# Masks added by a scaled identity on TensorE, one reduction for both heads, and q and k copied by twos in the first 16 units

## The chip, the core and the metric

The kernel runs on one core of one Trainium2 chip. The core has a matrix engine, TensorE (PE in the profile, PEld for its weight loads), and three engines for elementwise work: VectorE (DVE), ScalarE (ACT) and GpSimd (POOL). SyncE (SP) issues most of the transfers. Each engine takes its instructions in a fixed order and stands still at one whose input isn't there. Matmuls write to PSUM, a memory of eight banks per partition; the other data lie in SBUF. The metric is the device time of one execution in microseconds (us), lower is better.

## The reference

Attention with 4 batches, 8 heads, 768 positions and 64 channels per head, then a feed-forward layer with a rational activation. Per head h, with rel = i - j:

```python
scores = q @ k.T / sqrt(64)
is_global = j < n_global;  is_local = (rel >= 0) & (rel < n_local)     # 8 and 96
dist = n_local where global and not local, else |rel|
scores = scores - 2.0 ** -(h + 1) * dist, and -1e9 where neither global nor local
a = softmax(scores);  x = a @ v                     # x: 3072 tokens x 512
hid = x @ w_in                                      # 512 x 2048
g = (a0 + a1 hid + a2 hid^2 + a3 hid^3) / (1 + |b0| |hid| + |b1| hid^2 + 1e-6)
out = g @ w_out                                     # 2048 x 512
```

The weights come as 64-bit numbers, so each piece of 128x512 is fetched as 512 KB and decoded on the chip.

## The kernel before

**The work.** The 24 row blocks of 128 tokens are taken two at a time, a chunk of 256 tokens (c). A *unit* u is one pair of heads (p) of one row block; a chunk has 8 units, four pairs of its first row block and then four of its second. Since only 96 positions back and 8 global ones count, a unit looks at its own key block and the one before it; row block 0 of a batch (i = 0) has only its own. So a unit's scores are 128 x 2 heads x 256 keys, or 128 x 2 x 128 where i = 0. Units 0 to 3 have i = 0, units 4 to 15 have i = 1 to 3. Beside the units run *feed-forward steps* f, eight to a chunk, each for 256 hidden channels.

**A unit below 24 (PLAIN)** goes through these stages:

- `st_load`: q and k of two units are fetched into one tile `nat`, v into `vt`.
- `st_qkT`: PE transposes q and k of one unit into a PSUM tile `tk` (L389).
- `st_qkE`: ACT copies them to SBUF: q per head into `qz`, in the half of the partitions that belongs to the head, zeros in the other half (L402, scaled by 2^(h-2)), and k into `kF` (L404); where i = 0 also the 8 global keys into `kGF` (L406).
- `st_score`: PE multiplies per head into a PSUM tile `s` (L433, in fp32, which the trace shows as two records per matmul). DVE then adds a mask to the scores of each head, scales by -2^-(h+1), writes the result to the SBUF tile `pr` and takes its minimum along the row into `stats`, in one operation per head (L452). The mask holds minus the distance, and -1e30 where a key does not count. POOL copies the global keys over the next block's first columns (L440).
- `st_soft`: ACT takes the exponential of `pr` in place, with the minimum as bias, and sums the row (L462).
- `st_sums`, `st_norm`: DVE adds and inverts (L467, L469); from unit 8 on POOL scales `pr` (L478). For units 0 to 7 the inverse goes through PE instead (L511) and is multiplied in `st_x`.
- `st_pT`: PE transposes the probabilities into `tp` (L494), ACT copies them to SBUF (L497). `st_pv`: PE multiplies them with v into `o`, two units at a time (L520); `st_x` writes x (L541, L542, and from unit 8 on L549, L550).

The tiles `tk`, `s`, `tp` and `o` share three PSUM banks. `pl.qz` has three buffers.

**Beside it**, 32 weight pieces are fetched (L183, into six raw buffers that a decoding frees) and decoded by ACT (L202), POOL (L206) and DVE (L207, L209). The hidden matmuls of the first chunk are L263, with two records each, those of later chunks L271; the activation is L295 to L318 on ACT, POOL and DVE, its last operation L318; the output matmuls of the first chunk are L342, of later ones L347. L222 and L223 split decoded weights into two parts for the later chunks.

**The order** is made at build time by a scheduler from the priorities in `PRI` and `PRI_A`, from an estimate of how long things take, and from which of the buffers is free. So an edit of the early units also moves what stands beside them, on every engine.

Of the kernel before, what the change touches and what calls it, by code (L numbers as in the profile page):

```python
# [18 lines left out]
P = 128  # L19
G = 8  # L20
# [86 lines left out]
def tile_kernel(ctx: ExitStack, tc: tile.TileContext, q, k, v, n_global, n_local,  # L107
# [255 lines left out]
    ident_r = const.tile([P, P], FR, name="ident_r")  # L363
    mask0 = const.tile([P, P], BF16, name="mask0")
    masks = const.tile([P, 3, P], BF16, name="masks")
    sp = {}
# [9 lines left out]
    def st_qkT(u):  # L376
        p = unit(u)[2]
        if u >= PLAIN:
            tk = pl.ps_t.tile([P, 2, 2, P], FR, tag="t", name=f"tk{u}")
            for y in range(2):  # L380
                for z in range(2):
                    n = nat[u // 2][:, 1 - z, 2 * y:2 * y + 2, :]
                    nc.tensor.transpose(out=tk[:, y, z, :], in_=n.rearrange("p a d -> p (a d)"), identity=ident_r)  # L383
                tqk[u + y] = tk[:, y]
            return
        tk = pl.ps_t.tile([P, 2, P], F32, tag="t", name=f"tk{u}")
        for z in range(2):
            n = nat[u // 2][:, z, 2 * (p % 2):2 * (p % 2) + 2, :]
            nc.tensor.transpose(out=tk[:, z, :], in_=n.rearrange("p a d -> p (a d)"), identity=ident)  # L389
        tqk[u] = tk  # L390
# [4 lines left out]
    def st_qkE(u):  # L395
        c, t, p, b, i = unit(u)
        tk = tqk.pop(u)
        if u < PLAIN:
            qz = pl.qz[:, u % 3]
            for x in range(2):  # L400
# [25 lines left out]
    def st_score(u):  # L426
        c, t, p, b, i = unit(u)
        qT = qTs.pop(u)
        s_ps = pl.ps_t.tile([P, 2, 2, P], F32, tag="t", name=f"s{u}")
        for x in range(2):  # L430
            h = 2 * p + x
            if u < PLAIN:
                nc.tensor.matmul(out=blocks_of(s_ps[:, x], i), lhsT=qT[:, x, :], rhs=blocks_of(pl.kF[:, p], i),  # L433
# [10 lines left out]

        def mask(x):
            m0, m = (mask0, masks) if u < PLAIN or x == 0 else (pl.half0, pl.halves)
            return m0 if i == 0 else m[:, 0:2, :] if i % 2 else m[:, 1:3, :]
        pr = pl.att.tile([P, 2, 2, P], F32, tag="prob", name=f"pr{u}")
        st = stats[:, u % 4]
        for x in range(2):  # L450
            h = 2 * p + x
            nc.vector.tensor_tensor_reduce(  # L452
                out=blocks_of(pr[:, x], i), in0=blocks_of(s_ps[:, x], i), in1=mask(x),
                scale=-(2.0 ** -(h + 1 if u < PLAIN else 2 * p + 1)), scalar=3e38, op0=ALU.add, op1=ALU.min, accum_out=st[:, x:x + 1])
        prob[u] = (pr, st)

    def st_soft(u):
        i = unit(u)[4]
        pr, st = prob[u]
        for x in range(2):  # L460
            d = blocks_of(pr[:, x], i)
            nc.scalar.activation(out=d, in_=d, func=AF.Exp, scale=-1.0, bias=st[:, x:x + 1],  # L462
                                 accum_out=st[:, 2 + 2 * x:3 + 2 * x])

# [63 lines left out]
    def st_x(u0):  # L528
# [15 lines left out]
        xh, xl = xT[c]  # L544
        if u0 < DIVIDED:
            rs = pl.early.tile([P, 2, P], F32, tag="rs", name=f"rs{u0}", bufs=1)
            nc.scalar.copy(out=rs, in_=r)
            nc.vector.tensor_tensor(out=o, in0=o, in1=rs, op=ALU.mult)
        nc.scalar.copy(out=xh[:, ps, cs], in_=o)  # L549
# [6 lines left out]
    def windowed(lates):  # L556
# [4 lines left out]
        pl.kGF = pl.early.tile([P, NPAIR, G], F32, name="kGF")  # L561
        pl.qz = pl.early.tile([P, 3, 2, P], F32, name="qz")
        nc.scalar.dma_start(out=ni[:, 0:2], in_=n_local.bitcast(I32).partition_broadcast(1))
# [30 lines left out]
        for t in range(NU + LAG + F2 + 1):  # L594
# [32 lines left out]
            if t == PLAIN:  # L627
# [3 lines left out]
                pl.kG = pl.late.tile([P, H, G], FR, name="kG")  # L631
                pl.halves = pl.late.tile([P, 3, P], BF16, name="halves")
                pl.half0 = pl.late.tile([P, P], BF16, name="half0")
                tc.cur_priority = base + 1000 * t
                for m, full_m in ((pl.halves, masks), (pl.half0, mask0)):
                    nc.vector.tensor_scalar(out=m, in0=full_m, scalar1=0.5, scalar2=None, op0=ALU.mult)
                on("split", st_move, t)
            ffn("ffn1a", st_ffn1, f, 0)
            if t < PLAIN or t % 2 == 0:
                on("qkT", st_qkT, t)  # L640
# [198 lines left out]
```

## Time and profile before

| | |
|---|---|
| median of 3 runs | 750.11 us (749.84 to 750.31) |
| the profiled execution, whole | 750.29 us |
| its span, first to last instruction | 748.4 us |
| mean granted TensorE clock | 0.996 |
| TensorE busy | 724.8 us, 97% of the span |
| VectorE, ScalarE, GpSimd busy | 601.4, 576.9, 456.4 us |

How to read the rows of the prediction. A row of the stretches gives its bounds and length, then the busy time and number of instructions of PE, PEld, DVE, ACT and POOL, then the granted clock as a share of the full one, the busy share of the DMA engines and GB/s. A row of a timeline gives start, length (us), engine, line, operation, what it writes and reads, and in brackets how long the engine had been idle ahead of it and what ended that. Lengths of neighbours overlap, so the distance of two starts is what an operation holds its engine for. A row of a group gives line, operation, form and count, then total busy time and the mean of one in ns. The chain is followed back from the last instruction, always to what released it. Numbers at the end of tile names are left out in the profile: `w_3f` stands for the decoded pieces (3, 0) to (3, 3) and 3.

### The profile page before, as it was taken

The page shows a single profiled execution, that of the slowest core. Times are in us where ns is not written, and L with a number is a line of the kernel's source. Part 1 is how long each engine was busy: PE and PEld are TensorE (multiplying, and loading weights), DVE is VectorE, ACT ScalarE, POOL GpSimd, SP SyncE. Part 2 cuts the span into 40 slices and gives each one's busy share as a digit, 9 for nine tenths or more (in the row PEclk, how much of TensorE's full clock was granted, in tenths as well). Part 3 has the DMA queues.
Part 4 walks back from the last instruction along what each step waited for, and adds up shares of the span by engine and source line. Part 5 has one row for each costly group of instructions (what it writes and reads, how often), then busy time and mean ns, then how long its engine had stood idle before and what let it go on. Part 6 is the DMA issues. An engine that isn't in the chain of part 4 may idle for free.

```text
span 748.4 us, 15330 instructions
## 1 busy us (share of the span) xinstructions
PE 724.8 (97%) x5026; PEld 629.8 (84%) x5026; DVE 601.4 (80%) x1437; ACT 576.9 (77%) x1303; POOL 456.4 (61%) x504
## 2 busy tenths in 40 slices
PE   5898999999999999999999999999999999999996
PEld 4575667888988989999999999998988989998995
DVE  5889965888889797878888888887888888876565
ACT  6898576977987886877877878777877877866674
POOL 3384996776576675665756657656666566664441
PEclk9999999999999999999999999999999999999999
DMA  9986101123534443334434334334434333210000
GB/s 259 306 277 224 48 22 23 50 52 99 146 103 126 151 121 94 113 108 101 119 94 120 113 101 125 107 101 106 124 93 124 117 86 107 74 50 1 29 1 33
DMA packets 123581, 79.49 MB, mean 106 GB/s; under 512 B 82532, under 2 KB 104036, under 8 KB 123492
## 3 DMA queue, kind: packets, MB, share of 16 engines
q1 hardware_dynamic: 122288, 77.89, 36.4%
q8 instruction: 42, 0.69, 0.4%
q10 hardware_dynamic: 1204, 0.52, 0.3%
q14 instruction: 47, 0.39, 0.2%
HBM read 35.92 MB, written 6.29 MB: 56 GB/s over the span
## 4 chain that ended last, share of the span: by engine, by line
PE 90%; DVE 3%; DMA 3%; ACT 1%; issue 1%; SPq 0%; POOL 0%; DVEq 0%; ACTq 0%
PE h L271 34%; PE acc L347 32%; PE o L520 5%; PE s L438 5%; PE tp L494 4%; PE acc L342 3%; PE h L263 3%; PE s L433 2%; PE tk L383 1%; DMA r<-in_moe_w_in_dram 1%; DMA r<-in_moe_w_out_dram 1%; PE tk L389 1%; DMA nat<-in_q_dram 0%; DVE pr L452 0%; ACT pr L462 0%
## 5 line engine op out<-in xcount | busy, mean ns | idle before, releaser
L478 POOL TENSOR_SCALAR pr<-pr,stats 128x256 f32<-128x256 f32 (+1 forms) x176 | 156.3, 899 | 74.8 <-DVE stats L469 42.7
L271 PE MATMUL h<-xh,win_l 128*128 128x256 f32 x704 | 198.2, 282 | 0.0
L304 POOL TENSOR_TENSOR fa<-fa,fs 128x512 f32<-128x512 f32 x95 | 123.5, 1300 | 98.0 <-ACT fs L297 85.3
L347 PE MATMUL acc<-wout_l,g 128*128 128x512 f32 x352 | 139.3, 396 | 0.0
L271 PEld LDWEIGHTS h<-xh,win_l 128*128 128x128 f32 x704 | 133.1, 189 | 2.1 <-issue 1.2
L327 POOL TENSOR_TENSOR g<-fu,g 128x512 fp32r<-128x512 f32 x87 | 113.9, 1310 | 34.2 <-ACT g L326 22.8
L295 ACT ACTIVATE fu<-h,coef 128x512 f32<-128x512 f32 (+1 forms) x97 | 74.9, 772 | 45.0 <-PE h L271 39.8
L462 ACT ACTIVATE pr<-pr,stats 128x256 f32<-128x256 f32 (+1 forms) x192 | 92.9, 487 | 16.8 <-DVE stats L452 16.0
L311 ACT ACTIVATE fs<-fa,coef 128x512 f32<-128x512 f32 (+1 forms) x97 | 69.6, 718 | 30.0 <-POOL fa L304 28.4
L316 DVE SCALAR_TENSOR_TENSOR fu<-fu,coef,q 128x512 f32<-128x512 f32 (+1 forms) x97 | 71.6, 738 | 24.7 <-ACT q L312 23.3
L302 DVE TENSOR_TENSOR fu<-fu,h 128x512 f32<-128x512 f32 (+1 forms) x97 | 65.7, 677 | 30.5 <-ACT fs L297 27.9
L347 PEld LDWEIGHTS acc<-wout_l,g 128*128 128x128 f32 x352 | 66.2, 188 | 11.9
L415 ACT ACTIVATE kq<-tk 64x256 fp32r<-64x256 f32 x144 | 54.2, 377 | 26.6 <-DVE kq L416 15.1
L303 DVE SCALAR_TENSOR_TENSOR fu<-fu,coef,h 128x512 f32<-128x512 f32 (+1 forms) x97 | 71.7, 739 | 2.0
L317 DVE SCALAR_TENSOR_TENSOR q<-fa,coef,q 128x512 f32<-128x512 f32 (+1 forms) x97 | 72.1, 744 | 0.0
L497 DVE COPY pT<-tp 128x512 f32<-128x512 f32 (+1 forms) x75 | 48.4, 646 | 26.0 <-PE tp L494 25.1
L416 DVE SCALAR_TENSOR_TENSOR kq<-tk,kq 64x256 fp32r<-64x256 f32 x144 | 60.8, 423 | 8.6 <-ACT kq L415 4.2
L318 DVE SCALAR_TENSOR_TENSOR fu<-q,fu 128x512 f32<-128x512 f32 (+1 forms) x97 | 66.1, 682 | 1.6
L297 ACT ACTIVATE fs<-h,coef 128x512 f32<-128x512 f32 (+1 forms) x97 | 66.2, 683 | 1.5 <-DMA out_dram<-o 1.2
L296 ACT ACTIVATE fa<-h,coef 128x512 f32<-128x512 f32 (+1 forms) x97 | 65.5, 675 | 0.4 <-DMA out_dram<-o 0.4
L326 ACT CAST g<-fu 128x512 fp32r<-128x512 f32 (+1 forms) x89 | 54.9, 617 | 8.5 <-DVE fu L318 7.8
L312 ACT ACTIVATE q<-fs 128x512 f32<-128x512 f32 (+1 forms) x97 | 57.3, 591 | 2.2 <-DVE fu L318 0.7
(258 smaller groups left out, 2006.1 us busy)
## 6 DMA issues: line engine op xcount, KB each, us to landing
pm<-pr SPq DMA_DIRECT2D x60, 256.0 KB
mv<-nat SPq DMA_DIRECT2D x36, 256.0 KB
qT<-kq SPq DMA_DIRECT2D x144, 64.0 KB
r<-in_moe_w_in_dram SPq DMA_DIRECT2D x16, 512.0 KB
r<-in_moe_w_out_dram SPq DMA_DIRECT2D x16, 512.0 KB
nat<-in_q_dram SPq DMA_DIRECT2D x48, 128.0 KB
vt<-in_v_dram SPq DMA_DIRECT2D x48, 128.0 KB
nat<-in_k_dram SPq DMA_DIRECT2D x46, 128.0 KB
```

The costliest lines, as they stand in the source:

```text
L271: nc.tensor.matmul(out=hps[f][:, y, :], lhsT=w[:, fs], rhs=x[:, ct, :], start=(n == 0), stop=(n == 3 * NCT - 1))
L295: nc.scalar.activation(out=u, in_=h, func=AF.Identity, scale=a3, bias=a2)
L297: nc.scalar.activation(out=s, in_=h, func=AF.Square, scale=b1)
L303: nc.vector.scalar_tensor_tensor(out=u, in0=u, scalar=a1, in1=h, op0=ALU.add, op1=ALU.mult)
L304: side(f).tensor_tensor(out=a, in0=a, in1=s, op=ALU.add)
L311: nc.scalar.activation(out=s, in_=a, func=AF.Ln, bias=q1)
L316: nc.vector.scalar_tensor_tensor(out=u, in0=u, scalar=a0, in1=r, op0=ALU.add, op1=ALU.mult)
L317: nc.vector.scalar_tensor_tensor(out=r, in0=a, scalar=q1, in1=r, op0=ALU.add, op1=ALU.mult)
L327: side(f).tensor_tensor(out=g[:, 1, ys], in0=u, in1=g[:, 0, ys], op=ALU.subtract)
L347: nc.tensor.matmul(out=acc, lhsT=gs[f][:, z, y, ts], rhs=w, start=(ft == 0 and n == 0), stop=(ft == NFT - 1 and n == 2))
L462: nc.scalar.activation(out=d, in_=d, func=AF.Exp, scale=-1.0, bias=st[:, x:x + 1], accum_out=st[:, 2 + 2 * x:3 + 2 * x])
L478: nc.gpsimd.tensor_scalar(out=d, in0=d, scalar1=st[:, 6 + x:7 + x], scalar2=None, op0=ALU.mult)
```

## The change

For units 0 to 15 (`MASKED`):

- A bf16 tile `slope` holds four times the identity, times -2^-(2p+1). Per unit PE runs one matmul of it with the masks, 512 columns (256 where i = 0), which starts the accumulation in `s`; the two score matmuls are added to it. The masks now lie twice, whole for the first head and halved for the second, so the two operations at turn 24 that made the halves go to the start. q is scaled by -0.125 for all heads.
- DVE takes the minima of both heads in one `tensor_reduce` over `s`. ACT's exponentials read `s` in PSUM and write `pr`; before, they read and wrote `pr`.
- Four transposes of two units go into one PSUM tile; ACT copies q of two units in one operation per head, and k in one. The global keys are copied by POOL, for two pairs at once. `pl.qz` has four buffers.
- Three lines in `st_x` are removed that no unit reached. Units from 16 on keep their operations; units 16 to 23 find their mask under a new index.

```diff
+MASKED = 16
...
+        if u < MASKED:
+            tk = pl.ps_t.tile([P, 2, 2, P], F32, tag="t", name=f"tk{u}")
+            for y in range(2):
+                for z in range(2):
+                    n = nat[u // 2][:, z, 2 * y:2 * y + 2, :]
+                    nc.tensor.transpose(out=tk[:, z, y, :], in_=n.rearrange("p a d -> p (a d)"), identity=ident)
...
+        if u < MASKED:
+            n = u % 4
+            for x in range(2):
+                ds_ = slice(x * D, (x + 1) * D)
+                nc.scalar.activation(out=pl.qz[ds_, n:n + 2, x, :], in_=tk[ds_, 0], func=AF.Copy, scale=-0.125)
+            nc.scalar.copy(out=pl.kF[:, p:p + 2, i % 2, :], in_=tk[:, 1])
+            if i == 0:
+                nc.gpsimd.tensor_copy(out=pl.kGF[:, p:p + 2, :], in_=pl.kF[:, p:p + 2, 0, 0:G])
...
+        if u < MASKED:
+            m = masks[:, :, 0:2, :] if i % 2 else masks[:, :, 1:3, :]
+            nc.tensor.matmul(out=s_ps if i else s_ps[:, :, 0, :], lhsT=pl.slope[:, p, :], rhs=m if i else mask0,
+                             start=True, stop=False)
...
+                nc.tensor.matmul(out=blocks_of(s_ps[:, x], i), lhsT=qT[:, x, :], rhs=blocks_of(pl.kF[:, p], i),
+                                 start=False, stop=(x == 1))
...
+        if u < MASKED:
+            W = 2 if i else 1
+            nc.vector.tensor_reduce(out=st[:, 0:2], in_=s_ps[:, :, 0:W, :].rearrange("p x w k -> p x (w k)"),
+                                    op=ALU.min, axis=mybir.AxisListType.X)
...
-            d = blocks_of(pr[:, x], i)
-            nc.scalar.activation(out=d, in_=d, func=AF.Exp, scale=-1.0, bias=st[:, x:x + 1],
-                                 accum_out=st[:, 2 + 2 * x:3 + 2 * x])
+            nc.scalar.activation(out=blocks_of(pr[:, x], i), in_=blocks_of(src[:, x], i), func=AF.Exp, scale=-1.0,
+                                 bias=st[:, x:x + 1], accum_out=st[:, 2 + 2 * x:3 + 2 * x])
...
+        for p in range(NPAIR):
+            nc.scalar.mul(out=pl.slope[:, p, :], in_=ident, mul=-(2.0 ** -(2 * p + 1)))
...
+        for m in (mask0, masks):
+            nc.vector.tensor_scalar(out=m[:, 1], in0=m[:, 0], scalar1=0.5, scalar2=None, op0=ALU.mult)
```

What the scheduler made of it is shown at three places. Line numbers in the changed kernel are one higher for the weights and the activation (L207, L209, L318 become L208, L210, L319), and 31 to 36 higher behind `st_score`.

**VectorE at the decoding of weight piece 7 (w_out).** The tile `m` and `w_7f` are its two decode steps, `xl` the low part of x for units 8 and 9, `stats` the sums of unit 11. Before:

```order
L318 SCALAR_TENSOR_TENSOR fu_608<-q_662,fu_608 128x512
L550 TENSOR_TENSOR xl_701<-o_690,xh_700 128x2x128
L207 SCALAR_TENSOR_TENSOR m_715<-m_715,r_7_713 128x512
L209 SCALAR_TENSOR_TENSOR w_7f<-r_7_713,m_715 128x512
L207 SCALAR_TENSOR_TENSOR w_8f<-w_8f,r_8_782 128x512
L207 SCALAR_TENSOR_TENSOR w_9f<-w_9f,r_9_789 128x512
L209 SCALAR_TENSOR_TENSOR w_8f<-r_8_782,w_8f 128x512
```

Now:

```order
L476 TENSOR_REDUCE stats<-s_706 128x2
L208 SCALAR_TENSOR_TENSOR m_696<-m_696,r_7_694 128x512
L582 TENSOR_TENSOR xl_682<-o_671,xh_681 128x2x128
L210 SCALAR_TENSOR_TENSOR w_7f<-r_7_694,m_696 128x512
L503 TENSOR_REDUCE stats<-stats 128x2
L505 RECIPROCAL stats<-stats 128x2
L208 SCALAR_TENSOR_TENSOR w_8f<-w_8f,r_8_765 128x512
```

Both decode steps of piece 7 moved ahead of the sums of unit 11, and the first of them ahead of `xl`.

**VectorE ahead of the last elementwise operation of step 2.** `fu_756` before and `fu_739` now are the activation of feed-forward step 2, `fu_840` and `fu_817` that of step 3; `w_11f` to `w_15f` are decoded w_out pieces. Before:

```order
L302 TENSOR_TENSOR fu_840<-fu_840,h_820 128x512
L316 SCALAR_TENSOR_TENSOR fu_756<-fu_756,coef,q_831 128x512
L317 SCALAR_TENSOR_TENSOR q_831<-fa_757,coef,q_831 128x512
L222 CAST w_2_0h<-w_2_0f 128x512
L467 TENSOR_REDUCE stats<-stats 128x2
L209 SCALAR_TENSOR_TENSOR w_11f<-r_11_956,w_11f 128x512
L207 SCALAR_TENSOR_TENSOR w_12f<-w_12f,r_12_1029 128x512
L303 SCALAR_TENSOR_TENSOR fu_840<-fu_840,coef,h_820 128x512
L207 SCALAR_TENSOR_TENSOR w_13f<-w_13f,r_13_1036 128x512
L318 SCALAR_TENSOR_TENSOR fu_756<-q_831,fu_756 128x512
```

Now:

```order
L210 SCALAR_TENSOR_TENSOR w_11f<-r_11_935,w_11f 128x512
L317 SCALAR_TENSOR_TENSOR fu_739<-fu_739,coef,q_808 128x512
L318 SCALAR_TENSOR_TENSOR q_808<-fa_740,coef,q_808 128x512
L210 SCALAR_TENSOR_TENSOR w_12f<-r_12_1002,w_12f 128x512
L208 SCALAR_TENSOR_TENSOR w_14f<-w_14f,r_14_1081 128x512
L303 TENSOR_TENSOR fu_817<-fu_817,h_803 128x512
L505 RECIPROCAL stats<-stats 128x2
L503 TENSOR_REDUCE stats<-stats 128x2
L210 SCALAR_TENSOR_TENSOR w_13f<-r_13_1009,w_13f 128x512
L223 CAST w_0_0h<-w_0_0f 128x512
L208 SCALAR_TENSOR_TENSOR w_15f<-w_15f,r_15_1088 128x512
L319 SCALAR_TENSOR_TENSOR fu_739<-q_808,fu_739 128x512
```

The second decode steps of pieces 12 and 13, the first of 14 and 15 and the cast `w_0_0h` moved ahead of the last operation of step 2 (L318, now L319); the last-but-one operation of step 3 (L303, now L304) moved behind it.

**TensorE at the output matmuls of step 2** (`acc` from `w_4f` and `w_5f`). `h_973` before and `h_952` now are the hidden matmuls of step 5, `tp` transposed probabilities of unit 12, `s` the scores of unit 14. Before:

```order
L263 MATMUL h_973<-x_281,w_1_2f 128x256
L263 MATMUL h_973<-x_281,w_2_2f 128x256
L263 MATMUL h_973<-x_281,w_3_2f 128x256
L342 MATMUL acc_0_768<-w_4f,fu_756 128x512
L342 MATMUL acc_0_768<-w_5f,fu_756 128x512
L342 MATMUL acc_1_778<-w_4f,fu_756 128x512
L342 MATMUL acc_1_778<-w_5f,fu_756 128x512
L494 MATMUL tp_1007<-ident,pr_898 128x128 x2
```

Now:

```order
L530 MATMUL tp_918<-ident,pr_798 128x128 x2
L452 LDWEIGHTS slope
L452 MATMUL s_941<-masks,slope 128x512
L457 MATMUL s_941<-kF,qz 128x256 x2
L343 MATMUL acc_0_751<-w_4f,fu_739 128x512
L343 MATMUL acc_0_751<-w_5f,fu_739 128x512
L343 MATMUL acc_1_761<-w_4f,fu_739 128x512
L343 MATMUL acc_1_761<-w_5f,fu_739 128x512
L530 MATMUL tp_918<-ident,pr_798 128x128 x2
L264 MATMUL h_952<-x_278,w_0_2f 128x256
L264 MATMUL h_952<-x_278,w_1_2f 128x256
```

The hidden matmuls of step 5 moved from ahead of the output matmuls of step 2 to behind them.

On SP the fetches of w_out pieces 12, 13 and 14 (L183) moved ahead of a reload of the global rows of v (L524), which waits for value matmuls on PE; piece 15 still stands behind it.

More of the change, by code (lines that the diff above doesn't have):

```diff
@@ L363, in tile_kernel @@
     ident_r = const.tile([P, P], FR, name="ident_r")
-    mask0 = const.tile([P, P], BF16, name="mask0")
-    masks = const.tile([P, 3, P], BF16, name="masks")
+    mask0 = const.tile([P, 2, P], BF16, name="mask0")
+    masks = const.tile([P, 2, 3, P], BF16, name="masks")
     sp = {}
@@ L385, in st_qkT @@
             return
+        if u < MASKED:
[4 more added lines that the diff above has]
+                    nc.tensor.transpose(out=tk[:, z, y, :], in_=n.rearrange("p a d -> p (a d)"), identity=ident)
+            tqk[u] = tk
+            return
         tk = pl.ps_t.tile([P, 2, P], F32, tag="t", name=f"tk{u}")
@@ L397, in st_qkE @@
         tk = tqk.pop(u)
+        if u < MASKED:
[6 more added lines that the diff above has]
+                nc.gpsimd.tensor_copy(out=pl.kGF[:, p:p + 2, :], in_=pl.kF[:, p:p + 2, 0, 0:G])
+            for y in range(2):
+                qTs[u + y] = pl.qz[:, n + y]
+            return
         if u < PLAIN:
-            qz = pl.qz[:, u % 3]
+            qz = pl.qz[:, u % 4]
             for x in range(2):
@@ L443, in st_score @@
             nc.gpsimd.tensor_copy(out=pl.kq[:, hs, i % 2, 0:G], in_=pl.kG[:, hs, :])
-        def mask(x):
-            m0, m = (mask0, masks) if u < PLAIN or x == 0 else (pl.half0, pl.halves)
-            return m0 if i == 0 else m[:, 0:2, :] if i % 2 else m[:, 1:3, :]
+        st = stats[:, u % 4]
+        if u < MASKED:
+            W = 2 if i else 1
+            nc.vector.tensor_reduce(out=st[:, 0:2], in_=s_ps[:, :, 0:W, :].rearrange("p x w k -> p x (w k)"),
+                                    op=ALU.min, axis=mybir.AxisListType.X)
+            prob[u] = (s_ps, st)
+            return
         pr = pl.att.tile([P, 2, 2, P], F32, tag="prob", name=f"pr{u}")
-        st = stats[:, u % 4]
         for x in range(2):
             h = 2 * p + x
+            y = 0 if u < PLAIN else x
+            m = mask0[:, y] if i == 0 else masks[:, y, 0:2, :] if i % 2 else masks[:, y, 1:3, :]
             nc.vector.tensor_tensor_reduce(
-                out=blocks_of(pr[:, x], i), in0=blocks_of(s_ps[:, x], i), in1=mask(x),
+                out=blocks_of(pr[:, x], i), in0=blocks_of(s_ps[:, x], i), in1=m,
                 scale=-(2.0 ** -(h + 1 if u < PLAIN else 2 * p + 1)), scalar=3e38, op0=ALU.add, op1=ALU.min, accum_out=st[:, x:x + 1])
@@ L458, in st_soft @@
         i = unit(u)[4]
-        pr, st = prob[u]
+        src, st = prob[u]
+        pr = src
+        if u < MASKED:
+            pr = pl.att.tile([P, 2, 2, P], F32, tag="prob", name=f"pr{u}")
+            prob[u] = (pr, st)
         for x in range(2):
-            d = blocks_of(pr[:, x], i)
-            nc.scalar.activation(out=d, in_=d, func=AF.Exp, scale=-1.0, bias=st[:, x:x + 1],
-                                 accum_out=st[:, 2 + 2 * x:3 + 2 * x])
+            nc.scalar.activation(out=blocks_of(pr[:, x], i), in_=blocks_of(src[:, x], i), func=AF.Exp, scale=-1.0,
+                                 bias=st[:, x:x + 1], accum_out=st[:, 2 + 2 * x:3 + 2 * x])
     def st_sums(u):
@@ L544, in st_x @@
         xh, xl = xT[c]
[L545 to L548, printed above, removed]
         nc.scalar.copy(out=xh[:, ps, cs], in_=o)
@@ L561, in windowed @@
         pl.kGF = pl.early.tile([P, NPAIR, G], F32, name="kGF")
-        pl.qz = pl.early.tile([P, 3, 2, P], F32, name="qz")
+        pl.qz = pl.early.tile([P, 4, 2, P], F32, name="qz")
+        pl.slope = pl.early.tile([P, NPAIR, P], BF16, name="slope")
         nc.scalar.dma_start(out=ni[:, 0:2], in_=n_local.bitcast(I32).partition_broadcast(1))
@@ L585, in windowed @@
         scr = [scr[:, x, :] for x in range(4)]
-        window_masks(nc, scr, mask0, masks, nl, ng)
+        window_masks(nc, scr, mask0[:, 0], masks[:, 0], nl, ng)
+        for m in (mask0, masks):
+            nc.vector.tensor_scalar(out=m[:, 1], in0=m[:, 0], scalar1=0.5, scalar2=None, op0=ALU.mult)
         load_coef()
@@ L631, in windowed @@
                 pl.kG = pl.late.tile([P, H, G], FR, name="kG")
-                pl.halves = pl.late.tile([P, 3, P], BF16, name="halves")
-                pl.half0 = pl.late.tile([P, P], BF16, name="half0")
                 tc.cur_priority = base + 1000 * t
-                for m, full_m in ((pl.halves, masks), (pl.half0, mask0)):
-                    nc.vector.tensor_scalar(out=m, in0=full_m, scalar1=0.5, scalar2=None, op0=ALU.mult)
                 on("split", st_move, t)
             ffn("ffn1a", st_ffn1, f, 0)
-            if t < PLAIN or t % 2 == 0:
+            if MASKED <= t < PLAIN or t % 2 == 0:
                 on("qkT", st_qkT, t)
@@ L646, in windowed @@
                 pv(t - 8, 0)
-            if t < PLAIN:
+            if MASKED <= t < PLAIN or t < MASKED and t % 2 == 0:
                 on("qkE", st_qkE, t)
-            elif t % 2 == 0:
+            elif t >= PLAIN and t % 2 == 0:
                 on("qkE", st_qkE, t)
```

1 line of the change is left out of this document (added).

## Prediction

> **What bounds the kernel now.** I read the page's busy shares first, then the busy time by stretches, the chain that ended last, and the timelines of TensorE (PE), VectorE (DVE) and ScalarE (ACT) where the chain changes engine. The profiled execution took 750.29 us, 0.18 above the median of 750.11, with a span of 748.4 us and 1.9 us around it. The first row is the page's busy share; the others give, per stretch, its length and then busy time of PE, PEld, DVE, ACT and GpSimd (POOL), the granted clock and the DMA share.
>
> ```profile
> PE 724.8 (97%) x5026; PEld 629.8 (84%) x5026; DVE 601.4 (80%) x1437; ACT 576.9 (77%) x1303; POOL 456.4 (61%) x504
> 0.00:36.90 36.90, 25.58 (x134) 17.59 (x135) 25.80 (x103) 26.88 (x91) 11.39 (x33) 1.00 0.95 282
> 36.90:68.00 31.10, 31.05 (x180) 23.15 (x178) 26.96 (x65) 28.52 (x71) 21.71 (x30) 1.00 0.80 252
> 68.00:92.50 24.50, 19.61 (x74) 12.48 (x74) 24.50 (x46) 15.70 (x35) 19.48 (x18) 0.93 0.33 106
> 92.50:180.00 87.50, 87.47 (x528) 68.11 (x529) 67.86 (x149) 68.77 (x157) 67.78 (x63) 1.00 0.17 43
> ```
>
> Four regimes. Up to 36.9 us units 0 to 7 go through attention while the DMA engines are 95% busy with weights; PE is idle 11.3 us. From 36.9 to 68 PE is full. From 68 to 92.5 DVE is full (24.50 of 24.50) with weight decoding and the feed-forward's elementwise work, and PE waits. From 92.5 on PE is full almost to the end. All sixteen units of the change are scored ahead of 92.5. So the end is fixed by the moment at which PE is full for good, plus PE's work left at that moment; PE time added is paid unless it falls into one of PE's waits. The chain (start, length, what) shows the third regime, and PE's own timeline what it does there.
>
> ```profile
> 67.36 0.61 PE o L520 x8
> ...
> 68.71 5.16 DMA r<-in_moe_w_out_dram
> 73.89 0.69 ACT w_12f L202
> ...
> 91.87 0.61 DVE fu L318
> ...
> 92.53 3.70 PE acc L342 x8
> 71.59 1.13 PE L342 MATMUL acc<-w_2f,fu 128*128 128x512 f32 x2 [3.64 <-DVE fu L318]
> 72.55 1.69 PE L342 MATMUL acc<-w_3f,fu 128*128 128x512 f32 x2
> 74.03 1.91 PE L342 MATMUL acc<-w_2f,fu 128*128 128x512 f32 x2
> 76.82 3.62 PE L263 MATMUL h<-x,w_2f 128*128 128x256 f32 x16
> 83.08 3.72 PE L263 MATMUL h<-x,w_2f 128*128 128x256 f32 x16 [1.12 <-DVE fu L303]
> ```
>
> PE waited 3.64 us for the last elementwise step (L318) of feed-forward step 1, then took 76.82 - 71.59 = 5.23 us for eight records that take 3.70 at 92.53: 1.5 us lost to the lower clock (0.93 over the stretch).
>
> **Part by part. The mask matmuls (added, PE).** The trace has no bf16 matmul. The nearest rows are single-pass fp32r ones of the same widths, and for the upper end one fp32 score.
>
> ```profile
> 154.75 1.86 PE acc L347 x8
> 121.50 2.12 PE h L271 x18
> 60.53 0.86 PE s L433 x4
> 66.08 1.06 PE s L433 x4
> ```
>
> 1.86/8 = 0.233 us for 512 columns, 2.12/18 = 0.118 for 256. Four units (row block 0) need 256 columns, twelve 512: 4 x 0.118 + 12 x 0.233 = 3.3 us. I take that, since width and number of passes agree. The scores themselves cost 0.86 or 1.06 by what stood ahead, so a change of operand kind can cost 0.2 a unit: upper end 3.3 + 16 x 0.2 = 6.5; a lower end under 2 us is excluded, as no row streams 512 columns in less than half of 0.233. Where they lie: units 0 to 7 (4 x 0.118 + 4 x 0.233 = 1.4) in the 11.3 idle us ahead of 36.9; units 8 to 13 (1.4) in the full stretch, on the path; units 14 and 15 (0.5) in the DVE stretch, under PE's 4.9 us of idleness. If that cover is gone, they add 1.9. **Path: +1.4.**
>
> **The maxima (DVE).** Rows: start, length, what.
>
> ```profile
> 62.39 0.42 DVE L452 CUSTOM_DVE_ANT_0 pr<-s,masks 128x256 f32<-128x256 f32 x1
> ...
> 62.73 0.42 DVE L452 CUSTOM_DVE_ANT_0 pr<-s,masks 128x256 f32<-128x256 f32 x1
> ...
> 63.08 0.69 DVE L207 SCALAR_TENSOR_TENSOR w_3f<-w_3f,r 128x512 int32<-128x512 int32 x1
> 67.94 0.67 DVE L302 TENSOR_TENSOR fu<-fu,h 128x512 f32<-128x512 f32 x1
> 68.54 0.68 DVE L209 SCALAR_TENSOR_TENSOR w_3f<-r,w_3f 128x512 int32<-128x512 int32 x1
> ```
>
> Durations overlap, so starts are what count: two heads hold DVE from 62.39 to 63.08, 0.69 us. One reduction over 512 PSUM elements is not in the trace; L302 also reads 512 PSUM elements and holds DVE 0.60. Saving 0.09 a unit, between 0 and 0.35 (if a result two elements wide cost only one head's pass). Only units 12 to 15 fall into DVE's full stretch: **4 x 0.09 = -0.4**; the others save where DVE has gaps. [...]
>
> **Queries and keys (ACT).** The first three rows bound one unit's copies, the fourth is one exponential, the last two stand for the pair's wider copies.
>
> ```profile
> 56.46 0.54 ACT L402 ACTIVATE qz<-tk 64x128 f32<-64x128 f32 x2
> 57.01 0.27 ACT L404 COPY kF<-tk 128x128 f32<-128x128 f32 x1
> 57.18 0.38 ACT L549 CAST xh<-o 128x256 fp32r<-128x256 f32 x1
> 63.16 0.51 ACT L462 ACTIVATE pr<-pr,stats 128x256 f32<-128x256 f32 x1
> L415 ACT ACTIVATE kq<-tk 64x256 fp32r<-64x256 f32 x144 | 54.2, 377 | 26.6 <-DVE kq L416 15.1
> L541 ACT COPY x<-o 128x256 f32<-128x256 f32 x4 | 1.5, 370 | 1.4 <-PE o L520 1.4
> ```
>
> Now 0.72 us a unit (56.46 to 57.18), 1.44 a pair; then 2 x 0.377 + 0.37 = 1.12: 0.16 a unit saved. ACT is not full anywhere ahead of 92.5 (28.52 of 31.10 at most) and in the first stretch weights arrive no sooner, so I take 0, with 6 x 0.16 = 1.0 as the gain's end. The four slope operations come before the first transposes, four times a 0.27 us row, and ACT idles there:
>
> ```profile
> 5.65 0.57 ACT L402 ACTIVATE qz<-tk 64x128 f32<-64x128 f32 x2 [1.83 <-PE tk L389]
> ```
>
> 1.1 fits into 1.83. The halved masks, two short DVE operations moved ahead of the first score, can hold it up 0.8 us at most (L302's 0.60 for 512 columns scaled to 640), while weights set the pace; the four 8-column copies go to POOL, 31% busy there (11.39 of 36.90). All three: 0.
>
> **Score banks held longer.** A bank of scores came free after DVE's 0.69; now after 0.60 and two exponentials of 0.5, 0.9 us later, with three banks. Behind a waiting mask matmul all of PE is queued. Scores of two units in the full stretch start 5.5 us apart (60.53, 66.08), so I take 0; 1 us is the upper end.
>
> **The order.** The rows: DVE's one long gap ahead of its full stretch, a run of value matmuls, and two decode rows of the full stretch.
>
> ```profile
> 59.25 0.70 DVE L207 SCALAR_TENSOR_TENSOR m<-m,r 128x512 int32<-128x512 int32 x1 [1.23 <-ACT m L202]
> 65.49 0.59 PE o L520 x8
> 75.16 1.76 DVE L209 SCALAR_TENSOR_TENSOR w_10f<-r,w_10f 128x512 int32<-128x512 int32 x1
> 80.61 1.76 DVE L207 SCALAR_TENSOR_TENSOR w_12f<-w_12f,r 128x512 int32<-128x512 int32 x1
> ```
>
> (a) DVE decodes weight piece 7 now ahead of the place where it stood still, and three of the last four fetches no longer queue on SP behind the reload of the global values: the wait of 1.23 goes, **-1.2**, at worst 0 (late next: the arrival of w_out pieces 10 to 12). (b) On DVE five decode or cast operations of 0.6 us now stand ahead of step 2's last elementwise operation. (c) On PE the output matmuls of step 2 now stand ahead of step 5's hidden matmuls. What (b) and (c) do, followed in time: step 1's output matmuls start at 71.59 - 1.2 = 70.4; eight records (3.70), sixteen of step 4 (3.62), a mask and a unit's scores (0.23 + 1.06) bring PE to step 2's output matmuls at 79.0. DVE has, from step 1's last operation (done at about 70.3) to step 2's, 18 long operations of 0.6 and four short ones, 11.4 us: 81.7; if two rows are stretched as the two above are (1.76 for 0.69), 83.8. From there eight records (3.70, or 5.23 at the low clock), 0.4 of transposes (half of 0.86 for four narrow ones, an estimate) and twelve hidden records (12 x 3.62/16 = 2.7) bring PE to step 3's output matmuls at 88.5 or 92.1, against 92.53 now, but with work left over that is done by then today: two hidden matmuls (4 x 0.23 = 0.9), a run of value matmuls (0.59), a unit's scores (0.86) and its mask (0.23), 2.6. So the end moves by 88.5 + 2.6 - 92.5 = -1.4 or by +2.2, masks and all; beyond the terms above (1.4 - 0.4 - 1.2 = -0.2) that is -1.2 or +2.4. **I take the middle, +0.6**: DVE's rows were stretched in this stretch of before, yet not all of them.
>
> Sum: 1.4 - 0.4 - 1.2 + 0.6 = +0.4 us on 750.29, that is **750.7 us**.
>
> **Rivals.** *Slower: step 2's output matmuls become the wait.* The second line above, and DVE not starting 1.2 earlier after all: PE stands 5 us there, where its second wait was 1.12, and behind those matmuls nothing else on PE can run. +2.2 and up to 1.2 more; price +3 us, 753.3. For it: DVE's full 24.5 us and the two stretched rows. Against it: the operations removed from DVE and (a). It decides if step 2's result comes after about 83.
>
> [...]
>
> *Faster: the cover grows.* No decode row is stretched (-1.4) and ACT's 1.0 counts: -2.4, 747.9. For it: with the fetches issued ahead of a queued reload, POOL's part of decoding falls at other times than its additions. Against it: nothing in the order keeps them apart.
>
> *It does nothing visible:* weights arrive no sooner, each saving lies beside them, and 1.4 for the masks and 0.6 for the order are left: 752.3; inside the forecast's own range.
>
> **Chances.** Forecast 0.36 (own range 749.0 to 752.3), slower rival 0.30, faster rival 0.34. A measurement of this kernel can tell about 0.2%, 1.5 us, from no change. Faster by more: 0.33 of the faster rival and 0.02 of the forecast, 0.35. Slower by more: 0.28 and 0.05, 0.33. Within: 0.32. The range takes both rivals, and about 1 us beyond each for the unknown price of a change of operand kind and of stretching: 746.9 to 754.2.
>
> **What would show it.** Right, if mask matmuls take 0.23 us from start to start, the reduction 0.60, PE is full from 37 to 69 us and PE's wait at step 1's output matmuls is under 3 us with the clock at 1.00. The slower rival shows as a wait above 3 us of the step 2 output matmuls for DVE's last elementwise step; the faster one as PE full for good before 90 us with the same work left. Wrong altogether would be a PE wait at a mask matmul for an exponential, over and over.

## The result, and the profile after

The changed kernel took 755.11 us (median of 6 runs, 754.30 to 757.44) against 749.98 of the kernel before (6 runs, 749.07 to 750.92): ratio 1.0072, 95% interval 1.0058 to 1.0086. It is 5.1 us slower, outside the predicted range. The profiled execution took 755.08 us with a span of 753.3, 4.8 us more than that of before. First the page's busy shares, then the four stretches.

```profile
PE 726.8 (96%) x5042; PEld 632.4 (84%) x5042; DVE 600.3 (80%) x1389; ACT 574.3 (76%) x1279; POOL 457.8 (61%) x506
0.00:36.90 36.90, 26.63 (x153) 19.20 (x154) 26.85 (x83) 26.88 (x80) 12.68 (x36) 0.91 0.97 293
36.90:68.00 31.10, 27.29 (x161) 20.74 (x159) 27.20 (x49) 26.77 (x59) 23.97 (x30) 1.00 0.79 254
68.00:92.50 24.50, 19.28 (x64) 12.15 (x64) 23.75 (x39) 14.00 (x31) 18.27 (x17) 0.79 0.30 86
92.50:180.00 87.50, 87.50 (x521) 67.98 (x520) 62.43 (x137) 65.55 (x154) 63.88 (x60) 1.00 0.16 41
```

From 92.5 us on TensorE is as full as before. The loss lies ahead of that: the second stretch, full before (31.05 of 31.10), now has 3.8 idle us, and in the third the clock fell from 0.93 to 0.79. (In the first it fell from 1.00 to 0.91, which left no delay that shows at 58 us.) TensorE's timeline there, and then three rows of the kernel before:

```profile
58.43 1.02 PE L343 MATMUL acc<-w_0f,fu 128*128 128x512 f32 x2
...
66.09 0.66 PE L556 MATMUL o<-pT,vt 128*64 128x128 f32 x8 [1.68 <-ACT pT L533]
68.29 0.59 PE L452 MATMUL s<-masks,slope 128*128 128x512 bf16 x1 [1.54 <-ACT pT L533]
68.67 1.91 PE L457 MATMUL s<-kF,qz 128*128 128x256 f32 x4
70.51 1.12 PE L556 MATMUL o<-pT,vt 128*64 128x128 f32 x8
71.56 1.15 PE L343 MATMUL acc<-w_2f,fu 128*128 128x512 f32 x2
...
75.56 3.62 PE L264 MATMUL h<-x,w_2f 128*128 128x256 f32 x16
84.11 0.69 PE L530 MATMUL tp<-ident,pr 128*128 128x128 f32 x2 [4.93 <-POOL pr L514]
84.59 0.63 PE L452 MATMUL s<-masks,slope 128*128 128x512 bf16 x1
85.02 1.91 PE L457 MATMUL s<-kF,qz 128*128 128x256 f32 x4
86.72 1.91 PE L343 MATMUL acc<-w_4f,fu 128*128 128x512 f32 x2
88.43 1.17 PE L343 MATMUL acc<-w_5f,fu 128*128 128x512 f32 x2
...
91.15 0.38 PE L530 MATMUL tp<-ident,pr 128*128 128x128 f32 x2
91.37 2.75 PE L264 MATMUL h<-x,w_2f 128*128 128x256 f32 x12
93.96 0.60 PE L530 MATMUL tp<-ident,pr 128*128 128x128 f32 x4
94.40 1.02 PE L343 MATMUL acc<-w_6f,fu 128*128 128x512 f32 x2
```

```profile
61.45 1.02 PE L342 MATMUL acc<-w_0f,fu 128*128 128x512 f32 x2
...
86.64 1.02 PE L342 MATMUL acc<-w_4f,fu 128*128 128x512 f32 x2
...
90.07 0.38 PE L494 MATMUL tp<-ident,pr 128*128 128x128 f32 x2
```

Three places. TensorE came to step 0's output matmuls at 58.43, before at 61.45. Some 1.7 of these 3.0 us are work that the new order put behind them (two hidden records, one unit's scores and four transposes), so it was ahead by about 1.3. By step 1's output matmuls it had given all of that back (71.56; before 71.59), in two waits for ScalarE's copies and in rows at half pace behind them (granted clock 0.50 from 68.29 to 71.56 us). Then it waited 4.93 us for the normalized probabilities of unit 12 and ran the next 4 us at half pace (granted clock 0.50 from 84.11 to 88.11 us).

At the start of step 2's output matmuls both kernels stand level, 86.72 against 86.64. But the kernel before had the hidden matmuls of step 5 behind it; here they come later. What the changed kernel has more to do from there on: those sixteen records (83.08 to 86.64 before, 3.56 us), half of unit 12's transposes and unit 15's mask (0.2 each), and the output matmuls of step 2 themselves, which took 4.43 (86.72 to 91.15) instead of 3.43 (86.64 to 90.07). With the 0.08 between the starts that is 5.1, against the 4.8 between the profiled executions.

Why the transposes of unit 12 were late stands on VectorE (first four rows) and GpSimd (last row):

```profile
69.61 0.68 DVE L476 TENSOR_REDUCE stats<-s 128x2 f32<-128x512 f32 x1
70.22 0.68 DVE L319 SCALAR_TENSOR_TENSOR fu<-q,fu 128x512 f32<-128x512 f32 x1
...
75.28 0.14 DVE L503 TENSOR_REDUCE stats<-stats 128x2 f32<-128x4 f32 x1
...
82.21 0.15 DVE L505 RECIPROCAL stats<-stats 128x2 f32<-128x2 f32 x1
...
84.07 0.68 DVE L319 SCALAR_TENSOR_TENSOR fu<-q,fu 128x512 f32<-128x512 f32 x1
...
82.46 2.51 POOL L514 TENSOR_SCALAR pr<-pr,stats 128x256 f32<-128x256 f32 x2 [1.32 <-DVE stats L503]
```

Unit 12's reduction, sum and reciprocal take 1.0 us together and were spread from 69.61 to 82.36, because weight decoding stood between them in VectorE's fixed order. (The profile puts GpSimd's wait down to a sum, L503. It is that of unit 13, which ran right behind unit 12's reciprocal, from 82.28 to 82.41.) The last row but one is the last operation of step 2: it ended at 84.75 (before at 84.23). And on ScalarE, start, length and wait of four rows:

```profile
64.29 0.67 ACT L203 ACTIVATE w_10f<-r 128x512 f32<-128x512 f32 x1 [1.01 <-DMA r<-in_moe_w_out_dram]
...
65.47 0.56 ACT L533 COPY pT<-tp 128x512 f32<-128x512 f32 x1
66.52 0.66 ACT L203 ACTIVATE w_11f<-r 128x512 f32<-128x512 f32 x1 [0.49 <-DMA r<-in_moe_w_out_dram]
...
67.66 0.58 ACT L533 COPY pT<-tp 128x512 f32<-128x512 f32 x1
```

Both copies that TensorE waited for stood behind the decoding of pieces that were still on their way.

### The profile page after: what moved, and what is told of

It reads as the page before. It is cut to its first block, busy times and chain, and to the rows that moved or that the text cites. A ratio compares the mean times of both kernels' runs of the same rounds, so it can differ in the third digit from the quotient of the medians.

```text
span 753.3 us, 15278 instructions
## 1 busy us (share of the span) xinstructions
PE 726.8 (96%) x5042; PEld 632.4 (84%) x5042; DVE 600.3 (80%) x1389; ACT 574.3 (76%) x1279; POOL 457.8 (61%) x506
## 4 chain that ended last, share of the span: by engine, by line
PE 88%; DMA 4%; DVE 3%; ACT 2%; issue 1%; POOL 1%; SPq 0%; DVEq 0%; ACTq 0%; POOLq 0%
PE h L272 34%; PE acc L348 32%; PE o L556 5%; PE s L466 5%; PE tp L530 3%; PE acc L343 3%; PE h L264 3%; PE tk L384 1%; DMA r<-in_moe_w_in_dram 1%; DMA vt<-in_v_dram 1%; DMA r<-in_moe_w_out_dram 1%; PE s L461 1%; PE s L457 1%; POOL pr L514 0%; ACT pr L498 0%
## 5 line engine op out<-in xcount | busy, mean ns | idle before, releaser
L303 DVE TENSOR_TENSOR fu<-fu,h 128x512 f32<-128x512 f32 (+1 forms) x97 | 65.7, 678 | 33.3 <-ACT fs L298 31.1
L498 ACT ACTIVATE pr<-pr,stats 128x256 f32<-128x256 f32 (+1 forms) x160 | 77.6, 488 | 14.1 <-DVE stats L485 13.4
L304 DVE SCALAR_TENSOR_TENSOR fu<-fu,coef,h 128x512 f32<-128x512 f32 (+1 forms) x97 | 71.7, 739 | 2.0
L318 DVE SCALAR_TENSOR_TENSOR q<-fa,coef,q 128x512 f32<-128x512 f32 (+1 forms) x97 | 72.1, 744 | 0.0
L319 DVE SCALAR_TENSOR_TENSOR fu<-q,fu 128x512 f32<-128x512 f32 (+1 forms) x97 | 66.1, 682 | 1.5
L485 DVE CUSTOM_DVE_ANT_0 pr<-s,masks 128x256 f32<-128x256 f32 x136 | 52.3, 419 | 15.8 <-PE s L466 6.7
```

The costliest lines, as they stand in the source:

```text
L304: nc.vector.scalar_tensor_tensor(out=u, in0=u, scalar=a1, in1=h, op0=ALU.add, op1=ALU.mult)
L318: nc.vector.scalar_tensor_tensor(out=r, in0=a, scalar=q1, in1=r, op0=ALU.add, op1=ALU.mult)
L498: nc.scalar.activation(out=blocks_of(pr[:, x], i), in_=blocks_of(src[:, x], i), func=AF.Exp, scale=-1.0, bias=st[:, x:x + 1], accum_out=st ...
```

## The experiments

Theory O: the order that the scheduler made out of the changed program is the loss. Rivals: the work on TensorE (W), the copying by twos (Q), or, taken together, the operations themselves (P). Ratios are against the kernel before on the same chip, with their 95% intervals.

**Parts and shares of the change.** Four kernels, each in an order of the scheduler's own.

```diff
 # masks_alone: q and k of each unit by themselves, as before
-        if u < MASKED:
+        if u < 0:
             tk = pl.ps_t.tile([P, 2, 2, P], F32, tag="t", name=f"tk{u}")
...
-                               scale=float(2.0 ** (2 * p + x - 2)))
+                               scale=-0.125 if u < MASKED else float(2.0 ** (2 * p + x - 2)))
 # pairs_alone: the old masks and maxima
-        if u < MASKED:
+        if u < 0:
             m = masks[:, :, 0:2, :] if i % 2 else masks[:, :, 1:3, :]
 # masked8, masked12
-MASKED = 16
+MASKED = 8   # and 12
```

> The mask matmul and the single reduction for units 0 to 15, queries and keys of each unit transposed and copied by themselves as before. Theory O (the order): the loss comes from where VectorE's small softmax operations and step 2's last elementwise operation stand among the weight decoding, so that TensorE waits near 79 us. In this kernel's order the reciprocal of unit 12 stands directly ahead of step 2's last elementwise operation, some 15 long VectorE operations behind step 1's, and TensorE's transposes of unit 12 stand ahead of step 2's output matmuls: O expects a wait of 4 us or more at those transposes, about 754 to 756. Rival W (the work): the 16 mask matmuls, 3.3 us of TensorE, are paid at the end wherever they stand: 753.3. Rival Q (copying by twos delays the scores): 750 to 751.

Measured 762.82 us, 1.0169 (1.0156 to 1.0182). The wait that O forecast was there (5.69 us at unit 12's transposes), and another of 3.30 for ScalarE's key copies.

> Queries and keys copied by twos, masks and maxima on VectorE as before. All heads' queries are scaled by 0.125, so the scores of the heads are scaled otherwise than in the reference; the work is the same. Theory O: here the reciprocal of unit 12 stands right behind step 1's last elementwise operation, and step 2's last one some 10 long operations behind that (about 79 to 81 us), so TensorE has no wait above 2 us near 79 us: 748 to 750. Rival W: no mask matmuls, so as before, 750.0. Rival Q: most of the loss, 753 to 755.

Measured 754.24 us, 1.0045 (1.0031 to 1.0059).

> The whole change for units 0 to 7 alone; units 8 to 15 in the old form. Theory O: the reciprocal of unit 12 stands right behind step 1's last elementwise operation, step 2's last one about 14 long operations behind (80 to 81 us); a wait of 1 to 2 us at step 2's output matmuls: 749 to 751. Rival W: half of the units and the cheaper half of the matmuls (1.4 us): 751.4. Rival Q, half of the loss: 752.5.

Measured 754.51 us, 1.0058 (1.0042 to 1.0075).

> The whole change for units 0 to 11; units 12 to 15 in the old form. Theory O: the reciprocal of unit 12 stands again behind some 12 long VectorE operations, just ahead of step 2's last one, and the transposes of unit 12 ahead of step 2's output matmuls: a wait of 4 us at the transposes, 753 to 755, so a jump against the kernel with 8 units. Rival W: twelve units' matmuls, 2.3 us: 752.3, in line between 8 and 16 units. Rival Q: three quarters of the loss, 753.8.

Measured 753.96 us, 1.0042 (1.0027 to 1.0057).

W falls: the kernel without mask matmuls loses 3.4 us, the one with them alone 12.7, and 8, 12 and 16 units do not lie on a rising line. Q falls with the 12.7. O in the narrow form that I had given it falls too. Three of its four times missed; the fourth, with 12 units, was met without its wait (2.50 us at unit 12's transposes instead of 4, with waits of 3.08 and 2.47 ahead of it). In the kernels with pairs alone and with 8 units, TensorE's long wait was at step 1's output matmuls, 5.03 and 5.14 us, where the kernel before waited 3.64. But that is not where they lost. At step 3's output matmuls both stand level with the kernel before (92.39 and 91.96 us, before 92.53) with the same matmuls done, masks aside, but for two records; their last matmuls start 4.2 and 2.4 us later than before (the second in an execution of 752.72 us, 1.8 below its median). Both have waits behind that which the kernel before does not have, of up to 1 us each, between 168 and 243 us. Two rows with pairs alone:

```profile
73.00 2.08 PE L343 MATMUL acc<-w_2f,fu 128*128 128x512 f32 x2 [5.03 <-DVE fu L319]
...
240.87 0.35 PE L466 MATMUL s<-kq 128*128 128x256 f32 x1 [0.96 <-DVE stats L503]
```

These waits add up to less than the loss; what made the rest is open. What remains of O is wider: every edit gave another order, and each of these orders lost, at different places. That can be tested only by holding the order fixed.

**Operations against order.** Each instruction of the main loop got a name (stage, unit, number). The kernel then queues the instructions of each engine and of SP behind each other in a listed order; `free` is an edge that fixes the issue and waits for nothing.

```diff
+        by = {(a, e): i for a, e, i in labels}
+        for e, row in json.loads(zlib.decompress(base64.b85decode(ORDER))).items():
+            row = [by[a, e] for a in row]
+            for one, two in zip(row, row[1:]):
+                tc.add_manual_dep(two, one.name, free, reason="order")
```

> All operations of the changed kernel, with every instruction of the main loop put into the order that the kernel before has on each engine and queue (issue order alone, no added waits): a mask matmul directly ahead of its unit's first score matmul, the one reduction where the second head's maximum stood, the four transposes and three copies of a pair where those of its first unit stood. Theory O, in its wider form (the loss is made by the order alone, whatever the part that changed it): 749 to 751.5. Rival P (the operations themselves: TensorE's mask matmuls, score banks held until the exponentials, pairs copied together): as in the changed kernel, 754 to 756.

Measured 751.90 us (12 runs), 1.0027 (1.0018 to 1.0037).

> The reverse: every instruction in the order of the changed kernel, but masks and maxima as before, by two operations a unit on VectorE and a copy of the scores in SBUF; in place of the mask matmul stands one of 8 columns, so that the banks are taken in the same order. Queries and keys by twos; all heads scaled by 0.125, so scores are scaled otherwise than in the reference. Theory O: the loss stays, 753 to 756. Rival P: most of it goes with the masks' operations, 750 to 752.

Measured 757.15 us, 1.0100 (1.0085 to 1.0116).

> The kernel with masks and reduction alone, which took 762.8 us in the order of its own, in the order of the kernel before. Theory O: 749 to 751.5, 11 to 13 us less by order alone. Rival P: above 755.

Measured 751.13 us (11 runs), 1.0018 (1.0009 to 1.0027).

> The operations of the kernel before, with an 8-column matmul ahead of each score as a place holder, in the order that took 762.8 us. Theory O: 758 to 763. Rival P: 750 to 752.

Measured 761.40 us, 1.0154 (1.0141 to 1.0167).

The order decides most of it, both ways. The same operations went from 755.1 to 751.9 and from 762.8 to 751.1 us when only their order changed, and the old maxima in the two new orders stayed slow. In the order of the changed kernel the old maxima were rather slower than the new ones (1.0100 against 1.0072). No run holds the changed kernel's own order as it is, so what the listed order by itself does is seen in one case only, the copies by twos in the old order below (0.9992). The changed operations in the old order show TensorE's third stretch as the kernel before had it. The trace is of an execution of 749.59 us, one of the fastest of the twelve, so the 2 us that the median lost are not in it:

```profile
68.00:92.50 24.50, 20.01 (x77) 12.93 (x76) 24.50 (x39) 15.30 (x32) 20.12 (x18) 0.93 0.34 104
...
82.71 3.72 PE L479 MATMUL h<-x,w_2f 128*128 128x256 f32 x16 [1.20 <-DVE fu L519]
86.27 1.02 PE L558 MATMUL acc<-w_4f,fu 128*128 128x512 f32 x2
```

**Which places of the order.** The changed kernel in its own order, with single instructions moved in the list. The theories N, H and C each blame one place; the first expectation says which.

```diff
 # softmax12_early, VectorE and GpSimd
  d0_11.0
+ sums12.0 sums12.1
...
- sums12.0 ... sums12.1
 # GpSimd
+ norm12.0 norm12.1
  ew2_3.0
 # hidden5_first, TensorE and VectorE
+ ffn1a_5 (all) ffn1b_5 (all)
  pT12.0
...
  ew2_3.0
+ ew2_3.1
 # copies_first, ScalarE
+ pT10.0 pT11.0
  d0_10.0
```

> The changed kernel in its own order, but for unit 12's softmax: on VectorE the sum and the reciprocal of unit 12 stand four and eleven long operations earlier, right behind the first decode step of w_out piece 11, and GpSimd's normalization of unit 12 ahead of step 3's addition. Theory N (the 4.93 us wait for that normalization is the loss): TensorE goes on at 79.2 instead of 84.1 us, 750 to 751. Theory H (the loss is that the hidden matmuls of step 5, 3.6 us, stand behind the output matmuls of step 2; both kernels start those at 86.6 to 86.7, the one before with step 5's hidden matmuls done, and the changed one runs them at a low clock for another 1.0): the wait only moves to the output matmuls of step 2, whose input VectorE ends at 84.8; they start 1.9 earlier at most: 753 to 755. Theory C (the loss are the 1.7 and 1.5 us that TensorE waited near 65 and 67 us for ScalarE's copies of transposed probabilities): no change, 755.

Measured 754.71 us, 1.0058 (1.0045 to 1.0071). The wait moved to step 2's output matmuls, as theory H had it, and the clock fell there (0.72 from 68 to 92.5 us, 0.79 in the changed kernel). (The trace is of the slowest of six executions, 757.00 us.)

```profile
81.67 1.03 PE L672 MATMUL s<-kF,qz 128*128 128x256 f32 x4
86.69 2.07 PE L558 MATMUL acc<-w_4f,fu 128*128 128x512 f32 x2 [3.99 <-DVE fu L534]
88.55 1.91 PE L558 MATMUL acc<-w_5f,fu 128*128 128x512 f32 x2
```

> The changed kernel in its own order, but for step 5's hidden matmuls, which stand on TensorE ahead of unit 12's transposes instead of behind step 2's output matmuls, and for VectorE's last read of step 3's hidden bank, which stands right behind the operation ahead of it instead of behind step 2's last elementwise operation. Theory H: the hidden matmuls run from about 83 to 86.5 us in a wait that is there anyway, the output matmuls of step 2 start 1.3 to 1.6 later than in the changed kernel with 3.6 us less left: 752 to 753.5. Theory N: the normalization of unit 12 is as late as it was, but hidden behind other work, also about 752. Theory C: no change, 755.

Measured 754.00 us, 1.0045 (1.0032 to 1.0058), just above H's forecast: the hidden matmuls now stood behind a wait of 4.09 us and ran mostly at half pace (6.26 us, where these sixteen take 3.62 at full pace). (This trace too is of the slowest execution, 756.00 us.)

```profile
83.70 6.26 PE L479 MATMUL h<-x,w_2f 128*128 128x256 f32 x16 [4.09 <-DVE fu L519]
```

> Both moves: unit 12's softmax early, and step 5's hidden matmuls directly ahead of step 2's output matmuls, as in the kernel before. Theory H: transposes and scores done by 81, hidden matmuls from 83 to 86.5, output matmuls of step 2 from 86.6 at full clock, as in the kernel before: 749.5 to 751.5. Theory N: as with unit 12's softmax alone. Theory C: 755.

Measured 751.89 us (12 runs), 1.0022 (1.0010 to 1.0034), where the old order as a whole gave 1.0027. Both moves together recover 3.2 of the 5.1 us (3.7 by the ratios, where the first alone gave 1.0, which its interval does not tell from nothing, and the second 2.0). N, which had forecast 750 to 751 for the first move alone, and C, which had forecast 755 here, fall. H comes nearest but is just missed again: in the trace, of an execution of 753.8 us, the hidden matmuls had to wait once more and the output matmuls of step 2 started at 89.43, not at 86.6.

```profile
79.90 1.03 PE L672 MATMUL s<-kF,qz 128*128 128x256 f32 x4
84.19 5.41 PE L479 MATMUL h<-x,w_2f 128*128 128x256 f32 x16 [3.26 <-DVE fu L519]
89.43 1.02 PE L558 MATMUL acc<-w_4f,fu 128*128 128x512 f32 x2
```

> The changed kernel in its own order, but for ScalarE's two copies of the transposed probabilities of units 10 and 11, which stand ahead of its first decode step of w_out piece 10 (for whose transfer it waited 1.0 us) instead of behind it and behind that of piece 11. The two waits of TensorE near 65 and 67 us, 3.2 us, should fall by 2 us or more. Theory C: 752 to 753. Theories H and N: TensorE waits so much longer near 80 us, since VectorE and GpSimd are no earlier there: 754 to 756.

Measured 754.35 us, 1.0056 (1.0042 to 1.0070). The two waits near 65 us went, and 3.92 us of waiting came at step 1's output matmuls, which VectorE feeds:

```profile
70.78 2.08 PE L558 MATMUL acc<-w_2f,fu 128*128 128x512 f32 x2 [3.92 <-DVE fu L534]
...
83.84 0.69 PE L745 MATMUL tp<-ident,pr 128*128 128x128 f32 x2 [2.70 <-POOL pr L729]
```

**What is left.** Three runs on the 2 us that no order took away.

```diff
 # thin_in_old_order
-            nc.tensor.matmul(out=s_ps if i else s_ps[:, :, 0, :], lhsT=pl.slope[:, p, :], rhs=m if i else mask0,
-                             start=True, stop=False)
+            nc.tensor.matmul(out=s_ps[:, 0, 0, 0:8], lhsT=pl.slope[:, p, :], rhs=mask0[:, 0, 0:8],
+                             start=True, stop=True)
...
-                                 start=False, stop=(x == 1))
+                                 start=True, stop=True)
 # pairs_in_old_order: pairs_alone with the list of the kernel before
 # all_moves: both_moves and copies_first
```

> All operations of the changed kernel in the order of the kernel before, as in the run that took 751.9 us, but each mask matmul cut to 8 columns, which leaves the masks out of the scores and some 3 us of work out of TensorE; all else is the same. If TensorE pays for the mask matmuls of the stretch that is full (the prediction's 1.4 us): 750.2 to 750.8. If what is left of the loss comes from elsewhere: 751.5 to 752.

Measured 751.02 us (12 runs), 1.0011 (1.0002 to 1.0020). Cutting the mask matmuls took 0.0016 of the ratio, 1.2 us, though the two intervals overlap a little.

> Queries and keys copied by twos, masks and maxima on VectorE as before, in the order of the kernel before (754.2 us in an order of its own); all heads scaled by 0.125, so scores are scaled otherwise than in the reference. By the order alone: 749.5 to 750.5. If copying by twos costs what separates the two kernels with masks in the old order (751.9 and 751.1): 750.8.

Measured 749.36 us (12 runs), 0.9992 (0.9983 to 1.0002): no difference from the kernel before that this can tell. So what copying by twos lost in its own order, 3.4 us by the ratio, was order.

> The changed kernel with all three moves: unit 12's softmax early, step 5's hidden matmuls ahead of step 2's output matmuls, and ScalarE's copies of units 10 and 11 ahead of the decoding of piece 10. If VectorE sets the time of step 2's and step 3's results, the time that TensorE wins near 65 us is waited for near 80: 751 to 752.5. If the 3 us of waits near 65 us were paid: 749.

Measured 752.76 us, 1.0035 (1.0022 to 1.0047). No gain on both moves: what TensorE won near 65 us it waited for at step 1's output matmuls (3.72 us). No version beat the kernel before.

## Why the prediction was wrong

**The operations: right.** A mask matmul takes 0.23 us from start to start, and the scores behind it 1.03 as elsewhere, so the change of operand kind cost nothing:

```profile
22.99 0.39 PE L452 MATMUL s<-masks,slope 128*128 128x512 bf16 x1
23.22 1.03 PE L457 MATMUL s<-kF,qz 128*128 128x256 f32 x4
```

The reduction holds VectorE 0.61 from start to start (69.61 to 70.22; its row is 0.68 long); 0.60 was forecast. The masks' +1.4 on the path was 1.2 by the cut matmuls, though the intervals leave it anywhere from 0.2 to 2.2. The copies by twos, taken at 0, were at 0 in the old order. The halved mask held the first mask matmul up for 0.70 us at 6.7 us, within the 0.8 allowed; slope and global keys show in no wait of TensorE.

**Score banks held longer, taken at 0.** All operations in the old order lose 2.1 us, the cut masks 0.8. That 0.8 is the reduction, the exponentials from PSUM, the longer held banks, the 8-column matmuls and the listed order together. Which of them it is stays open. No repeated wait of a mask matmul for an exponential showed.

**(a), -1.2: the wait went, the gain did not last.** VectorE's gap ahead of piece 7 closed, and TensorE was some 1.3 us ahead at step 0's output matmuls. I let the 1.2 pass through to step 1's (70.4 forecast, 71.56 measured). Two things took it back: ScalarE's copies behind decoding that waited for transfers, which I had not looked at, and VectorE's step 1 result, at 70.90 instead of 70.3. That was 0.6 earlier than before (71.53) and not 1.2: VectorE had a new wait of 0.58 at the sums of unit 11, which now stand behind both decode steps, and a decode row at 63.58 took 1.76.

**(b) and (c), "I take the middle, +0.6": this step failed.** I followed TensorE to step 2's output matmuls at 79.0, past two transposes of unit 12 that stand ahead of unit 14's mask and scores in its order, as if they took nothing and their input were ready. TensorE was there at 79.2, but the probabilities that these transposes read hung on a reciprocal whose place on VectorE stands in the order above, and which I did not follow: a wait of 4.93 us, to 84.11. I had step 2's result at 81.7 or 83.8; it came at 84.75, 0.5 later than in the kernel before (84.23), where both of my cases had it earlier. From step 1's result VectorE took 13.85 us, where I had reckoned 11.4 or 13.5: not two decode rows were stretched but four (1.12 to 1.69 us, where others take 0.68). I let step 3's output matmuls start at 88.5 or 92.1; they started at 94.40. So even the upper of the two cases was 2.3 us short, and the middle between them had no case of its own.

**The slower rival had the place and the moment** (TensorE stands 5 us from 79; it decides if step 2's result comes after 83). The first releaser was another, the normalization of unit 12. With that out of the way the wait stood exactly where the rival put it, 3.99 us. Its price of 3 was too low. In the changed kernel step 2's output matmuls started at 86.72, not at 83.8 or 85: the result came at 84.75, and unit 12's transposes and unit 14's mask and scores, which I had done by 79.0, ran ahead of them only then, at half pace, from 84.11 to 86.72. Mending both places gave back 3.2 us; the other 2 are as much as the operations lose in the old order, which does not show that they are the same 2.

**What should have shown it right** was half there: the wait at step 1's output matmuls was gone, but TensorE was not full from 37 to 69 us, and the clock was not at 1.00.

**The clock.** The first of my two cases has TensorE wait 2.7 us at step 2's output matmuls (79.0 to 81.7) and then takes their eight records at 3.70, without a loss of clock. That was my estimate; no run had shown it. The runs showed half pace after waits of 2.12, 2.70 and 3.26 us and full pace after one of 3.04 (below); in the changed kernel even 1.54 us, not long after another 1.68, stood ahead of half pace (68.29, above). And the 1.5 us that I took for the loss behind the wait of 3.64 set the distance of starts (5.23) against a busy length (3.70). From start to start eight such records take 3.43 (86.64 to 90.07 before), so it was 1.8.

## What to carry to other kernels

Where a scheduler makes the order, time an edit twice: in its own new order, and with the old order pinned. Here the operations cost 2 us and the new order 3 more, and in one variant 11 more. Look for the loss over the whole execution: two of these orders lost theirs behind the stretch that had been edited. In a stretch where several engines are full, follow every input of the next instruction on the waiting engine, the tiny ones too: a reciprocal of 0.15 us held TensorE for 4.9. And removing one wait there pays only if the next input in line comes earlier too.

## What the runs showed of the hardware that was not expected

TensorE fell to half pace also after waits shorter than the 3.64 us of the kernel before: sixteen hidden records took 5.41 us instead of 3.62 after a wait of 3.26 (above) and also after one of 2.12 in the kernel with all moves, where the granted clock was 0.67 from 83.8 to 89.0 us. Transposes took 0.69 instead of 0.38 after one of 2.70. After 1.20 us the sixteen took 3.72. But length alone does not decide it: in the kernel with the old operations in the order that took 762.8 us, TensorE kept its full pace after a wait of 3.04 (granted clock 1.00 from 69 to 72 us). The first row is of the kernel with all moves, the others are of that one:

```profile
83.79 5.41 PE L479 MATMUL h<-x,w_2f 128*128 128x256 f32 x16 [2.12 <-DVE fu L519]
```

```profile
68.90 0.66 PE L737 MATMUL o<-pT,vt 128*64 128x128 f32 x8 [3.04 <-ACT kF L619]
...
69.53 1.11 PE L650 MATMUL s<-kF,qz 128*128 128x256 f32 x4
```

So 2.12 us of idleness were enough once, and 3.04 were not another time. What decides between them these runs do not show. Where the pace fell in the rows above, the sixteen hidden records cost 1.8 to 2.6 us on top of the wait (5.41 - 3.62 and 6.26 - 3.62); after the wait of 3.04 there was no such cost.
